# Eight experts in a written order, with whole-row gathers from a second copy of their input

## The chip, the core and the metric

The kernel runs on one NeuronCore of a Trainium2 chip. The metric is the device time of one execution in microseconds (us). The core has engines that each run their own queue of instructions: TensorE (PE in the profile; its weight loads are PEld), VectorE (DVE), ScalarE (ACT), GpSimd (POOL) and SyncE (SP), which here only issues DMAs. They wait for one another by semaphores. POOL issues the indirect DMAs, whose row numbers stand in SBUF.

## The reference

Block-causal attention over 4 x 8 heads of 576 x 64, a gated dense FFN on its 2304 rows of 512, and then eight experts. Everything is float32. The change touches the rows between the dense FFN and the output:

```python
def _moe2_ref(x, w_gate, w1, w2):          # x: 2304 x 512
    N, D = x.shape; E = w_gate.shape[1]    # E = 8
    cap = N // E                           # 288 tokens for an expert
    logits = x @ w_gate
    ...                                    # by falling logit: a token to the expert, while the expert has room
    out = np.zeros((N, D))
    for e in range(E):
        mask = assigned == e
        h = np.maximum(x[mask] @ w1[e], 0.0)   # 288 x 512 @ 512 x 1024
        out[mask] = h @ w2[e]                  # 288 x 1024 @ 1024 x 512
    return out
```

## The kernel before

Attention and the dense FFN's first half fill the span up to about 580 us, and the router, which decides the expert of every token, runs on DVE beside the FFN's second half. The FFN's second half (`A` of L683) leaves the experts' input, x2, as tiles `x2r`: ACT copies a group from PSUM with L690, and SP stores it by L692 to DRAM, in two arrays `x2_d[0]` and `x2_d[1]` of 2304 x 256, one for each half of a row. The last tiles hold one half row each, 128 x 256; so array 0 is complete one tile before array 1. When the router has written the table `idx`, the rows of an expert can be fetched.

**An expert** has 288 tokens, in pieces of 128, 128 and 32. `gather` (L997) fetches them with indirect DMAs on POOL, one per half row and piece: six for an expert. `xtrans` turns them on TensorE (L1009, three transposes for each of four slices `d` of the row) and splits each slice into a high part `exh{d}` (ACT, L1012) and a low part `exl{d}` (DVE); each product is made from three matmuls, high x high, low x high, high x low. The first layer has eight groups `f` (L1049), each of 12 matmuls with 288 columns, so 96 for an expert; ACT and DVE make `eh{f}` and `el{f}` of each. The second layer has four groups `d` of 24 (L1090), 96 too; ACT copies each to `yt{d}` (L1095). `ytrans` turns the four `yt` back on TensorE (L1023, 12 transposes), copies the three pieces to `yr` (ACT L1026, DVE L1028 twice), and sends them to their rows of the output with indirect DMAs on POOL (L1030).

The weights come in 64 loads through a ring (`eraw`, on SP's queue). `split` makes the high part `ewh` on ACT (L969) and the low part `ewl` in two halves, by turns on DVE (L974) and POOL (L976).

**Order.** `Experts.run` hands its instructions to a scheduler, which has its own estimates of costs and due times and may move an instruction ahead of others on its engine, within what the data allow. The first half of expert 0's slices (d = 0, 1) depends on `x2_d[0]` alone, and `early` starts five of its groups f with the six matmuls of these slices (30 in all, `EARLY`) ahead of the transposes for d = 2 and 3. The gathers of expert e+1 are written at the start of expert e. The transposes and scatters of expert e are the `tail` that is worked off beside the first layer of expert e+1.

Of the kernel before, what the change touches and what calls it, by code (L numbers as in the profile page):

```python
# [8 lines left out]
F32 = mybir.dt.float32  # L9
# [3 lines left out]
AF = mybir.ActivationFunctionType  # L13
OP = mybir.AluOpType
AX = mybir.AxisListType

P = 128
# [3 lines left out]
def f32(ap):  # L21
    return ap.bitcast(F32)
# [583 lines left out]
class Ffn2:  # L606
# [88 lines left out]
CAP = 288  # L695
# [228 lines left out]
        yield 0  # L924


EARLY = 5


class Experts:  # L930
# [27 lines left out]
    def split(self, eng):  # L958

        k, nc = self.k, self.k.nc  # L960
        if self.ns >= 64:
            return
        e, c = self.chunks[self.ns]
        self.ns += 1
        x = self.rawt.pop((e, c))
        h = self.ring.tile([P, 1024], F32R, name="ewh")
        l = self.ring.tile([P, 1024], F32R, name="ewl")
        self.w[e, c] = (h, l)
        nc.scalar.activation(h, x, AF.Copy)  # L969
        yield  # L970
        for a in range(2):
            s = slice(512 * a, 512 * a + 512)
            if eng == "v":
                nc.vector.tensor_tensor(l[:, s], x[:, s], f32(h[:, s]), op=OP.subtract)  # L974
            else:
                nc.gpsimd.tensor_tensor(l[:, s], x[:, s], f32(h[:, s]), op=OP.subtract)  # L976
            yield
        self.load()

# [4 lines left out]
    def open(self, st):  # L984
        tc = self.k.tc
        self.yg = st.enter_context(tc.tile_pool(name="yg", bufs=2))
        self.hb = st.enter_context(tc.tile_pool(name="ehb", bufs=1))

    def gather(self, e):
        k, nc = self.k, self.k.nc  # L990
        if e >= 8:
            return
        for c in range(2):
            for j, (a, b) in enumerate(self.TOK):
                if c == 0:
                    self.gx[e, j] = self.xg.tile([P, 512], F32, name=f"xg{j}")
                nc.gpsimd.indirect_dma_start(out=self.gx[e, j][0:b - a, 256 * c:256 * c + 256], out_offset=None, in_=k.x2_d[c][:, :],  # L997
                                             in_offset=bass.IndirectOffsetOnAxis(ap=k.idx[0:b - a, 3 * e + j:3 * e + j + 1], axis=0))

    def xtrans(self, e):  # L1000

        k, nc = self.k, self.k.nc
        if e >= 8:
            return
        parts = self.xt[e] = []
        for d in range(4):
            o = k.psA.tile([P, 512], F32, name="A")
            for j, (a, b) in enumerate(self.TOK):
                nc.tensor.transpose(o[:, a:b], self.gx[e, j][0:b - a, d * P:(d + 1) * P], k.ident[0:b - a, 0:b - a])  # L1009
            h = self.xg.tile([P, 288], F32R, name=f"exh{d}")  # L1010
            l = self.xg.tile([P, 288], F32R, name=f"exl{d}")
            nc.scalar.activation(h, o[:, 0:288], AF.Copy)  # L1012
            nc.vector.tensor_tensor(l, o[:, 0:288], f32(h), op=OP.subtract)
            parts.append((h, l))
            yield

    def ytrans(self, e, yt):
        k, nc = self.k, self.k.nc
        for j, (a, b) in enumerate(self.TOK):
            n = b - a  # L1020
            o = k.psA.tile([P, 512], F32, name="A")
            for d in range(4):
                nc.tensor.transpose(o[0:n, d * P:(d + 1) * P], yt[d][:, a:b], k.ident)  # L1023
            r = self.yg.tile([P, 512], F32, name=f"yr{j}")
            if j == 0:
                nc.scalar.activation(r[0:n], o[0:n], AF.Copy)  # L1026
            else:
                nc.vector.tensor_copy(r[0:n], o[0:n])  # L1028
            yield
            s = nc.gpsimd.indirect_dma_start(out=k.out[:, :], out_offset=bass.IndirectOffsetOnAxis(  # L1030
                ap=k.idx[0:n, 3 * e + j:3 * e + j + 1], axis=0), in_=r[0:n, :], in_offset=None)
            for x in self.sent:
                k.tc.declare_no_dep(s.ins, x.ins, reason="no token is in two slots")
            self.sent.append(s)
            yield

    def run(self):
        k, nc = self.k, self.k.nc
        nxt = self.xtrans(0)
        tail, bg = iter(()), iter(())  # L1040
        early = {}

        def first(o, e, f, ds):
# [8 lines left out]
        next(nxt)  # L1052
        for f in range(EARLY):
            early[f] = k.psF.tile([P, 512], F32, name="A")
            first(early[f], 0, f, (0, 1))
        drain(nxt)
        for e in range(8):
            self.gather(e + 1)
            hs = []
            for f in range(8):  # L1060
# [15 lines left out]
                next(bg, None)  # L1076
            yt = []
            nxt = self.xtrans(e + 1)
            for d in range(4):
                drain(bg)  # L1080
                bg = self.split("v" if d % 2 == 1 else "g")
                next(bg, None)
                wh, wl = self.w[e, 4 + d]
                o = k.psF.tile([P, 512], F32, name="A")
                n = 0
                for f in range(8):
                    s = slice(P * f, P * f + P)
                    h, l = hs[f]
                    for w, x in ((wh, h), (wh, l), (wl, h)):
                        nc.tensor.matmul(o[:, 0:288], w[:, s], x, start=(n == 0), stop=(n == 23))  # L1090
                        n += 1
                    if f in (3, 5):
# [4 lines left out]
                if d >= 1:  # L1097
                    next(nxt, None)
            drain(nxt)
            drain(tail)  # L1100
            tail = self.ytrans(e, yt)
            yield
        drain(tail)


# [4 lines left out]
def drain(g):  # L1110
    for _ in g:
        pass
# [54 lines left out]
def tile_fn(ctx, tc, q, kk, v, w_gate, w_val, w_out, m_gate, w1, w2, out, dbg=None):  # L1167
    nc = tc.nc
    nb = 4
    k = K()  # L1170
    k.nc, k.tc, k.ctx, k.q, k.kk, k.v, k.nb = nc, tc, ctx, q, kk, v, nb
    k.w_gate, k.w_val, k.w_out, k.m_gate, k.w1, k.w2, k.out = w_gate, w_val, w_out, m_gate, w1, w2, out
    dram = ctx.enter_context(tc.tile_pool(name="dram", bufs=1, space=bass.MemoryType.DRAM))
    k.h_d = [dram.tile([P, 12, 576], F32, name=f"h{b}") for b in range(nb)]
    k.wgv_d = dram.tile([12, 2, P, 512], F32, name="wgv")
    k.wo_d = dram.tile([12, P, 512], F32, name="wo32")
    k.x2_d = [dram.tile([2304, 256], F32, name=f"x2d{c}") for c in range(2)]
# [28 lines left out]
    ex = Experts()  # L1206
# [10 lines left out]
    with tc.manual_schedule():  # L1217
        n = 0
# [46 lines left out]
```

## Time and profile before

| | us |
|---|---|
| three runs | 1047.32, 1046.84, 1045.98 (median 1046.84) |
| profiled execution | 1045.71 |
| its span, first to last instruction | 1044.0 |
| PE busy | 993.2 (95%) |
| DVE, ACT, POOL busy | 587.7, 449.7, 507.4 |
| mean granted clock of TensorE, as a share of full | 0.985 |

How to read it: the span and what lies around it (1.7 us) make the profiled execution's time. TensorE is busy nearly throughout, so the places that matter are those where it isn't, or where it is busy at a lower granted clock. Nearly the whole stretch from 785 us to the end belongs to the experts. In a row of the timeline, the bracket at the end holds the time that the engine was idle just before, and what ended it: an engine, tile and line, a DMA, "remote" (something that the profile couldn't place) or "issue" (nothing that the profile shows).

### The profile page before, as it was taken

What the parts mean: (1) busy time and instruction counts of PE and PEld (TensorE: products, weight loads), DVE (VectorE), ACT (ScalarE), POOL (GpSimd) and SP (SyncE); (2) the same over time, 40 slices, a digit from 0 to 9 for tenths busy, and PEclk for the clock granted to TensorE, in tenths of its full rate; (3) what the DMA queues carried; (4) which work ended last, traced back from release to release, by engine and by line L of the source; (5) the groups of instructions that cost most, each with busy time, mean ns of one, the idle gap of its engine ahead of it and who ended that gap; (6) DMA issues with size and microseconds to landing.
All of it is one profiled execution on the core that took longest, in us unless ns stands there. A gap on an engine that the chain in (4) does not pass through costs nothing.

```text
span 1044.0 us, 19724 instructions
## 1 busy us (share of the span) xinstructions
PE 993.2 (95%) x7387; PEld 858.1 (82%) x7387; DVE 587.7 (56%) x1385; ACT 449.7 (43%) x1069; POOL 507.4 (49%) x519
## 2 busy tenths in 40 slices
PE   7979999999999999999999999999997999999995
PEld 4658888788888888899999766666687999999995
DVE  5887889477666455435685566655631434434441
ACT  5765565355554455434554222111121444444541
POOL 3663444433333334532324677765645666666441
PEclk9989999999999999998999999999998999999998
DMA  6556666556454322236665543433312665555540
GB/s 170 141 130 176 203 199 178 181 165 185 142 184 119 96 68 79 75 98 226 207 210 157 148 126 102 119 84 96 98 47 63 205 186 174 177 169 183 185 127 23
DMA packets 188527, 148.89 MB, mean 143 GB/s; under 512 B 70800, under 2 KB 161424, under 8 KB 188432
## 3 DMA queue, kind: packets, MB, share of 16 engines
q1 hardware_dynamic: 184848, 138.20, 44.5%
q0 software_dynamic: 3584, 9.44, 2.8%
q8 instruction: 58, 0.95, 0.4%
q14 instruction: 37, 0.30, 0.1%
HBM read 114.57 MB, written 33.03 MB: 141 GB/s over the span
## 4 chain that ended last, share of the span: by engine, by line
PE 84%; DVE 8%; issue 4%; POOL 1%; ACT 1%; SPq 1%; DMA 0%; POOLq 0%; another core or an unknown queue 0%; ACTq 0%; DVEq 0%
PE A L457 29%; PE A L683 12%; PE A L1049 10%; PE A L1090 9%; PE A L211 5%; PE A L116 4%; PE A L163 4%; PE A L824 2%; PE A L410 2%; DVE sub L811 2%; PE A L122 2%; PE A L1009 1%; PE A L85 1%; DVE cmp L840 1%; DVE hl L512 1%
## 5 line engine op out<-in xcount | busy, mean ns | idle before, releaser
L151 POOL TENSOR_SCALAR p<-p,stat 128x128 f32<-128x128 f32 (+2 forms) x144 | 81.2, 576 | 191.1 <-DVE stat L149 135.8
L359 POOL TENSOR_TENSOR w0l<-wf,w0h 128x512 fp32r<-128x512 f32 x48 | 67.0, 1395 | 136.9 <-ACT w0h L357 103.4
L457 PE MATMUL A<-xh,w0h 128*128 128x288 f32 x384 | 121.6, 317 | 2.6 <-ACT w0h L357 2.6
L457 PE MATMUL A<-xh,w1h 128*128 128x288 f32 x384 | 122.1, 318 | 1.9 <-ACT ptb L168 1.9
L976 POOL TENSOR_TENSOR ewl<-eraw,ewh 128x512 fp32r<-128x512 f32 x68 | 90.2, 1345 | 63.1 <-ACT ewh L969 55.6
L457 PE MATMUL A<-xh,w0l 128*128 128x288 f32 x384 | 114.5, 298 | 3.7 <-POOL w0l L359 3.7
L457 PE MATMUL A<-xh,w1l 128*128 128x288 f32 x384 | 114.3, 298 | 0.0
L457 PE MATMUL A<-xl,w1h 128*128 128x288 f32 x384 | 114.3, 298 | 0.0
L457 PE MATMUL A<-xl,w0h 128*128 128x288 f32 x384 | 114.1, 297 | 0.0
L969 ACT ACTIVATE ewh<-eraw 128x1024 fp32r<-128x1024 f32 x64 | 67.8, 1060 | 67.2 <-PE A L1090 42.0
L124 DVE TENSOR_REDUCE stat<-A 128x1 f32<-128x128 f32 (+4 forms) x160 | 70.4, 477 | 44.2 <-PE A L122 20.5
L683 PE MATMUL A<-wo_h,hl 128*128 128x512 f32 (+1 forms) x240 | 95.0, 396 | 0.0
L683 PE MATMUL A<-wo_l,hh 128*128 128x512 f32 (+1 forms) x240 | 92.1, 384 | 0.0
L660 POOL TENSOR_TENSOR hl<-hraw,hh 128x512 fp32r<-128x512 f32 x54 | 75.8, 1426 | 28.7 <-ACT hh L656 28.7
L683 PE MATMUL A<-wo_h,hh 128*128 128x512 f32 (+1 forms) x240 | 89.7, 374 | 0.0
L974 DVE TENSOR_TENSOR ewl<-eraw,ewh 128x512 fp32r<-128x512 f32 x60 | 48.6, 851 | 70.8 <-ACT ewh L969 64.9
L138 ACT ACTIVATE p<-A,stat 128x128 f32<-128x128 f32 (+4 forms) x160 | 81.8, 520 | 11.7 <-DVE stat L124 7.5
L690 ACT ACTIVATE x2r<-A 128x512 f32<-128x512 f32 (+1 forms) x20 | 11.1, 555 | 168.2 <-PE A L683 162.6
L1049 PE MATMUL A<-exh,ewh 128*128 128x288 f32 x256 | 75.9, 314 | 6.0 <-issue 3.3
L457 PEld LDWEIGHTS A<-xh,w1h 128*128 128x128 f32 x384 | 73.5, 191 | 9.0 <-issue 5.1
L457 PEld LDWEIGHTS A<-xh,w0h 128*128 128x128 f32 x384 | 73.1, 190 | 8.7 <-issue 4.4
L1049 PE MATMUL A<-exl,ewh 128*128 128x288 f32 x256 | 75.8, 299 | 2.3 <-issue 2.3
(219 smaller groups left out, 2717.1 us busy)
## 6 DMA issues: line engine op xcount, KB each, us to landing
eraw<-in_moe_w_dram SPq DMA_DIRECT2D x64, 512.0 KB, 3.9
wf<-wgv SPq DMA_DIRECT2D x72, 256.0 KB, 3.0
h<-h SPq DMA_DIRECT2D x48, 288.0 KB, 2.7
hraw<-h SPq DMA_DIRECT2D x16, 768.0 KB, 5.2
hraw<-h SPq DMA_DIRECT2D x12, 576.0 KB, 4.0
w<-in_moe_w_gate_dram SPq DMA_DIRECT2D x12, 512.0 KB, 4.3
w<-in_moe_w_val_dram SPq DMA_DIRECT2D x12, 512.0 KB, 4.1
wgv<-wf SPq DMA_DIRECT2D x24, 256.0 KB, 4.3
```

Of the source, the lines that this page charges most:

```text
L124: nc.vector.tensor_reduce(st[:, x:x + 1], s[:, 0:w], axis=AX.X, op=OP.max, negate=True)
L138: nc.scalar.activation(o, s[:, 0:w], AF.Exp, bias=m, scale=1.0, accum_out=st[:, 2 + x:3 + x])
L151: self.k.mark = nc.gpsimd.tensor_scalar(t, t, r[:, x:x + 1], 1.0, op0=OP.mult, op1=OP.mult)
L211: nc.tensor.matmul(o[64 * a:64 * a + 64, b0:w], vs[0:kk, c, a, :], th[0:kk, a, c, b0:w], start=(n == 0), stop=(n == len(mm) - 1))
L359: nc.gpsimd.tensor_tensor(l, x, f32(h), op=OP.subtract)
L457: nc.tensor.matmul(o[:, 0:288], w[:, ks], x[:, ts], start=(kk == 0 and n == 0), stop=(kk == 3 and n == 2))
L660: nc.gpsimd.tensor_tensor(l[:, s], x[:, s], f32(h[:, s]), op=OP.subtract)
L683: nc.tensor.matmul(o[:, 0:b - a], x[:, f], w[:, f, a:b], start=(f == 0 and n == 0), stop=(f == 11 and n == 2))
L969: nc.scalar.activation(h, x, AF.Copy)
L976: nc.gpsimd.tensor_tensor(l[:, s], x[:, s], f32(h[:, s]), op=OP.subtract)
L1049: nc.tensor.matmul(o[:, 0:288], w[:, s], x, start=(d == 0 and n == 0), stop=(d == 3 and n == 2))
L1090: nc.tensor.matmul(o[:, 0:288], w[:, s], x, start=(n == 0), stop=(n == 23))
```

## The change

- Each tile `x2r` is stored twice: by halves to `x2_h[0]`, `x2_h[1]` (the former `x2_d`), and whole to the new `x2_d` of 2304 x 512.
- Only expert 0 is gathered by halves, six DMAs. Experts 1 to 7 are gathered by whole rows, three DMAs each.
- `EARLY` is 6: 36 matmuls of expert 0 go ahead of the transposes of its slices 2 and 3.
- The experts run under `manual_schedule`: every engine gets its instructions as they are written. So the groups f are no longer interleaved, the four transposes of a piece stand together behind the groups f = 0, 1, 2, and the three transposes of a slice for the next expert stand behind the 12th matmul of a group d.
- The weight splits have new places: five of eight on DVE and three on POOL, before four and four.
- `rows` takes the place of `ytrans`. A memset of one element on POOL stands between the scatters of a piece. For the last expert, the transposes of yt0 to yt2 with their copies (384 columns) go into the middle of the last group d; behind the last matmul come three transposes, copies of 128 columns and the scatters.

```diff
-                nc.sync.dma_start(k.x2_d[c // 256][t * P:(t + 1) * P, :], y[:, c - a:c - a + 256])
+                nc.sync.dma_start(k.x2_h[c // 256][t * P:(t + 1) * P, :], y[:, c - a:c - a + 256])
+            nc.sync.dma_start(k.x2_d[t * P:(t + 1) * P, a:b], y[:, 0:b - a])
...
-EARLY = 5
+EARLY = 6
...
-        for c in range(2):
+        self.gx[e] = [self.xg.tile([P, 512], F32, name=f"xg{j}") for j in range(3)]
+        for src in k.x2_h if e == 0 else (k.x2_d,):
             for j, (a, b) in enumerate(self.TOK):
...
+                g = self.gx[e][j][0:b - a]
+                if e == 0:
+                    c = k.x2_h.index(src)
+                    g = g[:, 256 * c:256 * c + 256]
+                nc.gpsimd.indirect_dma_start(out=g, out_offset=None, in_=src[:, :],
...
-    def ytrans(self, e, yt):
+    def rows(self, e, yt, ds, copies):
...
+        lo, hi = ds[0] * P, ds[-1] * P + P
         for j, (a, b) in enumerate(self.TOK):
+            o = self.yo[j]
+            for d in ds:
+                nc.tensor.transpose(o[0:b - a, d * P:(d + 1) * P], yt[d][:, a:b], k.ident)
+            r = self.yr[j][0:b - a]
             if j == 0:
+                nc.scalar.activation(r[:, lo:hi], o[0:b - a, lo:hi], AF.Copy)
             else:
+                nc.vector.tensor_copy(r[:, lo:hi], o[0:b - a, lo:hi])
+            if copies:
+                if j:
+                    nc.gpsimd.memset(self.one, 0.0)
+                s = nc.gpsimd.indirect_dma_start(out=k.out[:, :], ...
...
             for f in range(8):
+                if f % 2 == 0:
+                    drain(bg)
+                    if e or f:
+                        bg = self.split("vg"[f // 2 % 2])
+                    next(bg, None)
...
-                if f % 2 == 1:
-                    drain(bg)
-                    bg = self.split("v" if f % 4 == 1 else "g")
...
-                bg = self.split("v" if d % 2 == 1 else "g")
+                bg = self.split("gv"[d % 2] if d else "v")
...
+                    if f == 3:
+                        next(nxt, None)
+                        if e == 7 and d == 3:
+                            drain(self.rows(e, yt, (0, 1, 2), False))
...
-            tail = self.ytrans(e, yt)
-            yield
+            tail = self.rows(e, yt, range(4) if e < 7 else (3,), True)
...
-    ex.gather(0)
-    drain(ex.run())
+    with tc.manual_schedule():
+        ex.gather(0)
+        ex.run()
```

What follows are pieces of the engines' orders; a name with its number is one tile. First POOL before, from the start of the gathers: x2d_63 and x2d_64 are the arrays of the first and of the second half row; xg_9782, 9784 and 9786 are the pieces of expert 0, xg_9858, 9860 and 9862 those of expert 1.

```order
L997 DMA xg_9782<-x2d_63,idx 128x256
L997 DMA xg_9784<-x2d_63,idx 128x256
L997 DMA xg_9786<-x2d_63,idx 32x256
L997 DMA xg_9858<-x2d_63,idx 128x256
L997 DMA xg_9860<-x2d_63,idx 128x256
L997 DMA xg_9862<-x2d_63,idx 32x256
L997 DMA xg_9782<-x2d_64,idx 128x256
L997 DMA xg_9784<-x2d_64,idx 128x256
L997 DMA xg_9786<-x2d_64,idx 32x256
L997 DMA xg_9858<-x2d_64,idx 128x256
```

And the same place now, with x2h_64 and x2h_65 for the halves and x2d for the whole rows; xg_9806 to 9808 are expert 0's, xg_9889 to 9891 expert 1's:

```order
L1000 DMA xg_9806<-x2h_64,idx 128x256
L1000 DMA xg_9807<-x2h_64,idx 128x256
L1000 DMA xg_9808<-x2h_64,idx 32x256
L1000 DMA xg_9806<-x2h_65,idx 128x256
L1000 DMA xg_9807<-x2h_65,idx 128x256
L1000 DMA xg_9808<-x2h_65,idx 32x256
L1000 DMA xg_9889<-x2d,idx 128x512
L1000 DMA xg_9890<-x2d,idx 128x512
L1000 DMA xg_9891<-x2d,idx 32x512
L974 TENSOR_TENSOR ewl<-eraw,ewh 128x512 x6
```

Expert 0's second halves have moved ahead of all of expert 1's; and the 18 gathers that stood in a row (six more for expert 2 behind those shown) have become nine, with expert 0's six weight halves between them and expert 2's.

POOL before at the start of an expert (expert 1; gathers for the expert after the next one's start, then the scatters of the expert that has ended):

```order
L997 DMA xg_10527<-x2d_63,idx 128x256
L997 DMA xg_10527<-x2d_64,idx 128x256
L997 DMA xg_10529<-x2d_63,idx 128x256
L997 DMA xg_10531<-x2d_63,idx 32x256
L997 DMA xg_10529<-x2d_64,idx 128x256
L997 DMA xg_10531<-x2d_64,idx 32x256
L1030 DMA out_dram<-yr_10193,idx 2304x512
L1030 DMA out_dram<-yr_10240,idx 2304x512
L976 TENSOR_TENSOR ewl<-eraw,ewh 128x512 x2
L1030 DMA out_dram<-yr_10289,idx 2304x512
L976 TENSOR_TENSOR ewl<-eraw,ewh 128x512 x6
```

And now:

```order
L1000 DMA xg_10542<-x2d,idx 128x512
L1000 DMA xg_10543<-x2d,idx 128x512
L1000 DMA xg_10544<-x2d,idx 32x512
L1040 DMA out_dram<-yr_10571,idx 2304x512
L1039 MEMSET one 1x1
L1040 DMA out_dram<-yr_10572,idx 2304x512
L1039 MEMSET one 1x1
L1040 DMA out_dram<-yr_10573,idx 2304x512
L974 TENSOR_TENSOR ewl<-eraw,ewh 128x512 x6
```

Eight indirect DMAs in a row have become four, then one and one with a memset ahead of each, and the weight halves all stand behind the third scatter.

TensorE at the end of the program before, from the last matmuls of expert 7 on:

```order
L1090 MATMUL A_12610<-el7_12525,ewh_12490 128x288
L1090 MATMUL A_12610<-eh7_12524,ewl_12491 128x288
L1023 MATMUL A_12637<-ident_71,yt0_12554 128x128
L1023 MATMUL A_12637<-ident_71,yt1_12581 128x128
L1023 MATMUL A_12637<-ident_71,yt2_12608 128x128
...
L1023 MATMUL A_12637<-ident_71,yt3_12635 128x128
L1023 MATMUL A_12645<-ident_71,yt3_12635 128x128
L1023 MATMUL A_12653<-ident_71,yt3_12635 32x128
```

And now:

```order
L1031 MATMUL A_12642<-ident_72,yt0_12571 32x128
L1031 MATMUL A_12642<-ident_72,yt1_12598 32x128
L1031 MATMUL A_12642<-ident_72,yt2_12625 32x128
L1107 MATMUL A_12627<-eh4_12484,ewh_12507 128x288
...
L1107 MATMUL A_12627<-eh7_12541,ewl_12508 128x288
L1031 MATMUL A_12640<-ident_72,yt3_12670 128x128
L1031 MATMUL A_12641<-ident_72,yt3_12670 128x128
L1031 MATMUL A_12642<-ident_72,yt3_12670 32x128
```

Nine of the twelve transposes have moved from behind the last matmul to 12 matmuls ahead of it.

## Rows read from the trace of the kernel before

**Rows 1.** Two stretches: busy PE, PEld, DVE, ACT, POOL; granted clock; DMA share; GB/s.
```profile
780.00:800.00 20.00, 15.09 (x99) 14.17 (x98) 1.74 (x4) 2.31 (x6) 13.43 (x16) 0.88 0.28 85
1004.00:1031.00 27.00, 27.00 (x204) 26.68 (x205) 9.00 (x18) 9.39 (x19) 5.36 (x5) 1.00 0.20 62
```

**Rows 2.** Timeline of TensorE around the start.
```profile
784.33 0.28 PE L683 MATMUL A<-wo_h,hl 128*128 128x256 f32 x1
784.46 1.10 PE L1009 MATMUL A<-ident,xg 128*128 128x128 f32 x6
...
794.86 0.62 PE L1009 MATMUL A<-ident,xg 128*128 128x128 f32 x4
```

**Rows 3.** Timeline of ACT around the start: start, us, instruction, idle before.
```profile
780.38 0.39 ACT L690 ACTIVATE x2r<-A 128x256 f32<-128x256 f32 x1 [3.93 <-PE A L683]
786.34 0.38 ACT L690 ACTIVATE x2r<-A 128x256 f32<-128x256 f32 x1 [5.57 <-PE A L1009]
787.78 0.71 ACT L1012 ACTIVATE exh<-A 128x288 fp32r<-128x288 f32 x2 [1.06 <-remote]
797.23 0.41 ACT L1012 ACTIVATE exh<-A 128x288 fp32r<-128x288 f32 x1 [8.74 <-remote]
```

**Rows 4.** The chain that ended last, first layer of expert 0: start, us, what.
```profile
788.25 5.76 PE A L1049 x30
...
795.48 2.22 issue
797.70 6.80 PE A L1049 x37
804.50 0.52 issue
...
805.31 0.40 issue
...
808.87 4.28 PE A L1090 x32
```

**Rows 5.** Timeline of POOL: gathers at the start, and expert 1's run of eight.
```profile
779.07 1.20 POOL L997 DMA_INDIRECT xg<-x2d,idx  x1 [8.08 <-DMA x2d<-x2r]
...
785.53 0.87 POOL L997 DMA_INDIRECT xg<-x2d,idx  x1 [0.30 <-issue]
788.71 0.97 POOL L997 DMA_INDIRECT xg<-x2d,idx  x1 [2.31 <-DMA x2d<-x2r]
...
853.82 0.99 POOL L997 DMA_INDIRECT xg<-x2d,idx  x1 [1.00 <-PE A L1009]
```

**Rows 6.** Timeline of ACT during that run of eight.
```profile
857.20 0.60 ACT L1026 ACTIVATE yr<-A 128x512 f32<-128x512 f32 x1 [2.40 <-issue]
...
861.02 0.41 ACT L1069 ACTIVATE eh<-A 128x288 fp32r<-128x288 f32 x1 [3.22 <-PE A L1049]
```

**Rows 7.** The same chain, experts 1, 6 and 7.
```profile
823.80 0.99 PE A L1049 x6
...
975.60 0.99 PE A L1049 x6
...
985.02 4.74 PE A L1049 x36
...
1004.68 0.99 PE A L1049 x6
```

**Rows 8.** All x2 stores of L692, from issue to landing.
```profile
DMA to landing us min/median/max: 1.7/1.8/2.7
```

**Rows 9.** All gathers of L997, in ns (min/median/max).
```profile
L997 POOL DMA_INDIRECT xg<-x2d,idx x48: 864/954/1314, 779.1 to 951.6; - x48
```

**Rows 10.** Timeline of all engines behind the last matmul.
```profile
1031.63 1.47 PE L1023 MATMUL A<-ident,yt 128*128 128x128 f32 x12
1032.92 0.60 ACT L1026 ACTIVATE yr<-A 128x512 f32<-128x512 f32 x1 [0.62 <-PE A L1023]
...
1033.79 0.99 POOL L1030 DMA_INDIRECT out_dram<-yr,idx  x1 [16.68 <-ACT yr L1026]
```

More of the change, by code (lines that the diff above doesn't have):

```diff
@@ L972, in split @@
             s = slice(512 * a, 512 * a + 512)
[L973 to L976, printed above, removed]
+            (nc.vector if eng == "v" else nc.gpsimd).tensor_tensor(l[:, s], x[:, s], f32(h[:, s]), op=OP.subtract)
             yield
@@ L987, in open @@
         self.hb = st.enter_context(tc.tile_pool(name="ehb", bufs=1))
+        self.one = self.hb.tile([1, 1], F32, name="one")
     def gather(self, e):
@@ L992, in gather @@
             return
-        for c in range(2):
+        self.gx[e] = [self.xg.tile([P, 512], F32, name=f"xg{j}") for j in range(3)]
+        for src in k.x2_h if e == 0 else (k.x2_d,):
             for j, (a, b) in enumerate(self.TOK):
-                if c == 0:
-                    self.gx[e, j] = self.xg.tile([P, 512], F32, name=f"xg{j}")
-                nc.gpsimd.indirect_dma_start(out=self.gx[e, j][0:b - a, 256 * c:256 * c + 256], out_offset=None, in_=k.x2_d[c][:, :],
+                g = self.gx[e][j][0:b - a]
[3 more added lines that the diff above has]
+                nc.gpsimd.indirect_dma_start(out=g, out_offset=None, in_=src[:, :],
                                              in_offset=bass.IndirectOffsetOnAxis(ap=k.idx[0:b - a, 3 * e + j:3 * e + j + 1], axis=0))
@@ L1008, in xtrans @@
             for j, (a, b) in enumerate(self.TOK):
-                nc.tensor.transpose(o[:, a:b], self.gx[e, j][0:b - a, d * P:(d + 1) * P], k.ident[0:b - a, 0:b - a])
+                nc.tensor.transpose(o[:, a:b], self.gx[e][j][0:b - a, d * P:(d + 1) * P], k.ident[0:b - a, 0:b - a])
             h = self.xg.tile([P, 288], F32R, name=f"exh{d}")
@@ L1015, in xtrans @@
             yield
-    def ytrans(self, e, yt):
+    def rows(self, e, yt, ds, copies):
         k, nc = self.k, self.k.nc
+        if not self.yo:
+            self.yo = [k.psA.tile([P, 512], F32, name="A") for _ in self.TOK]
+            self.yr = [self.yg.tile([P, 512], F32, name=f"yr{j}") for j in range(3)]
+        lo, hi = ds[0] * P, ds[-1] * P + P
         for j, (a, b) in enumerate(self.TOK):
[L1020 to L1024, printed above, removed]
+            o = self.yo[j]
+            for d in ds:
+                nc.tensor.transpose(o[0:b - a, d * P:(d + 1) * P], yt[d][:, a:b], k.ident)
+            r = self.yr[j][0:b - a]
             if j == 0:
-                nc.scalar.activation(r[0:n], o[0:n], AF.Copy)
+                nc.scalar.activation(r[:, lo:hi], o[0:b - a, lo:hi], AF.Copy)
             else:
-                nc.vector.tensor_copy(r[0:n], o[0:n])
-            yield
[L1030 to L1034, printed above, removed]
-            yield
+                nc.vector.tensor_copy(r[:, lo:hi], o[0:b - a, lo:hi])
+            if copies:
+                if j:
+                    nc.gpsimd.memset(self.one, 0.0)
+                s = nc.gpsimd.indirect_dma_start(out=k.out[:, :], out_offset=bass.IndirectOffsetOnAxis(
+                    ap=k.idx[0:b - a, 3 * e + j:3 * e + j + 1], axis=0), in_=r, in_offset=None)
+                for x in self.sent:
+                    k.tc.declare_no_dep(s.ins, x.ins, reason="no token is in two slots")
+                self.sent.append(s)
+            yield
+        if copies:
+            self.yo = []
     def run(self):
         k, nc = self.k, self.k.nc
+        self.yo = []
         nxt = self.xtrans(0)
-        tail, bg = iter(()), iter(())
+        tail = iter(())
         early = {}
@@ L1059, in run @@
             hs = []
+            bg = iter(())
             for f in range(8):
+                if f % 2 == 0:
[3 more added lines that the diff above has]
+                    next(bg, None)
                 if f in early:
@@ L1072, in run @@
                 next(tail, None)
-                if f % 2 == 1:
-                    drain(bg)
-                    bg = self.split("v" if f % 4 == 1 else "g")
                 next(bg, None)
+            drain(tail)
             yt = []
@@ L1091, in run @@
                         n += 1
-                    if f in (3, 5):
+                    if f in (1, 5):
                         next(bg, None)
+                    if f == 3:
+                        next(nxt, None)
+                        if e == 7 and d == 3:
+                            drain(self.rows(e, yt, (0, 1, 2), False))
                 y = self.hb.tile([P, 288], F32, name=f"yt{d}")
@@ L1096, in run @@
                 yt.append(y)
-                if d >= 1:
-                    next(nxt, None)
+            drain(bg)
             drain(nxt)
-            drain(tail)
-            tail = self.ytrans(e, yt)
-            yield
+            tail = self.rows(e, yt, range(4) if e < 7 else (3,), True)
         drain(tail)
@@ L1176, in tile_fn @@
     k.wo_d = dram.tile([12, P, 512], F32, name="wo32")
-    k.x2_d = [dram.tile([2304, 256], F32, name=f"x2d{c}") for c in range(2)]
+    k.x2_d = dram.tile([2304, 512], F32, name="x2d")
+    k.x2_h = [dram.tile([2304, 256], F32, name=f"x2h{c}") for c in range(2)]
     const = k.const = ctx.enter_context(tc.tile_pool(name="const", bufs=1))
```

## The prediction

> **What bounds the kernel now.** I read three views: busy time by stretches, the chain of waits from the experts' start to the end, and the timelines of ACT and POOL where that chain leaves TensorE. From 1004 to 1031, the last expert, TensorE is busy 27.00 of 27.00 us at granted clock 1.00; between 780 and 800 it is busy 15.09 of 20 at 0.88 [rows 1]. So an expert in full swing is bound by TensorE itself, and time can be had at the start, in what makes experts 1 to 5 slower than expert 6, and behind the last matmul.
>
> The start: the last matmul of the dense FFN ends at 784.6 [rows 2]. ACT's x2r before it came at 780.38; the last one should follow at 784.7 and comes at 786.34, with ACT idle for 5.57 [rows 3]. TensorE gets to the experts at 788.25, waits 2.22 at 795.48, and has two gaps later (0.52, 0.40); the first layer ends at 808.87 [rows 4]. Both waits are odd. Transposes end at 795.48, but ACT's exh follows at 797.23, and the profile names no releaser ("remote") [rows 2, 3]. Each time POOL is deep in a run of indirect DMAs with 0.30 between two: the first six run from 779.07 to 786.40, the moment at which x2r moves; twelve more begin at 788.71 [rows 5]. I read from it that **after some five indirect DMAs in an unbroken run, TensorE's signals reach the other engines 1 to 2.7 us late**, and TensorE is held up too.
>
> The same in the middle: expert 1's run of eight begins at 853.82 [rows 5]. ACT's yr at 857.20, 3.4 into it, has 2.40 of idle; eh at 861.02, 7.2 into it, has 3.22 [rows 6]. Experts 1 to 5 take (975.60 - 823.80) / 5 = 30.36 each; expert 6, which gathers nothing (there is no expert 8), takes 29.08 [rows 7].
>
> **The change, part by part.** The sum is made against the profiled execution, 1045.71.
>
> *T1, the start to the end of expert 0's first layer.* POOL now issues three gathers and waits for the second half's last store. They end at 779.07 + 3 x 1.25 = 782.8, so POOL rests when the FFN ends: x2r at 784.7, stored from 785.1 instead of 786.72. The transposes' signal is prompt too: exh0 at 785.1 to 785.5, then exl0, which the written order now asks for with the second matmul (before, exh alone was used first): stream from 786.0. 36 early matmuls at full clock take 4.74, 0.132 each [rows 7]: 790.7. [...] The second half: its store goes 1.62 earlier, so its gathers too, from 788.71 [rows 5] to 787.1; the third is issued by 790.5 and lands about 1.1 later (an estimate, from 1.8 between issue and landing of a store [rows 8] less its own 0.9 in a gather's issue), 791.6. Six transposes (0.6) and the split of a slice (0.4 + 0.4): second layer-halves from 792.6. That leaves a wait of about 1.3 apart from the transposes. Then 96 - 36 = 60 matmuls x 0.132 = 7.9, 800.5; I keep the two later gaps (0.92), since six gathers still stand in a run there: about 801.5, so **T1 = 801.5 - 808.87 = -7.4**. Bounds: if nothing becomes prompt, only the sixth group is gained (six matmuls, 0.8, that fill part of the 2.22): -0.8; without the gaps kept, -8.3.
>
> *T2, expert 0's second layer* (808.87 to 823.80 [rows 4, 7]): the same matmuls and transposes, 0 (0 to -0.3).
>
> *T3, experts 1 to 5.* POOL's run at an expert's start falls from eight to four (three whole-row gathers, one scatter), some 5 us, then single scatters with a memset ahead of each. A whole-row gather fetches as many rows as a half-row one, each twice as long; I price it as before, 954 ns in the middle [rows 9]; the trace has no gather of 2 KB rows but scatters of such rows, 0.99 each [rows 10]. If all the excess over expert 6 goes: 5 x 29.08 - 151.80 = -6.4. I take -5.5, since a run of four still reaches five us. Below: nothing, 0, if the run isn't the cause. Matmuls and transposes are equal in number. Strict order is covered: ahead of the first group's use of exh3 stand 12 matmuls of d = 3 and nine of the group, 21 x 0.132 = 2.8, against 0.8 for ACT and DVE. POOL's split written at f = 2 stands behind the third scatter, which waits for the copy of the third piece behind f = 2 (36 matmuls and 12 transposes, 4.7 + 1.5 [rows 7, 10]); with copy, scatter and 2.6 for two halves it is done some 11 us into the expert, and its weights are used in d = 1, 96 x 0.132 + 1.5 + 3.5 = 17.7 into it. The memsets ride in that slack.
>
> [...]
>
> *T4, the tail.* Nine of the last 12 transposes move ahead of 12 matmuls. All 12 took 1.47 [rows 10], so nine put 1.0 into the stream before its end: +1.0. Behind the last matmul yt3's copy is as before; the first scatter came 1033.79 - 1032.92 = 0.87 after the copy of 512 columns (0.60) began [rows 10]. 128 columns should take 0.3: -0.3. yt3's copy starts when the last matmul ends whatever stood behind it, and nine transposes lay beside that copy before; so they were hidden: -0.2 for the shorter way to yt3. **T4 = +0.5** (from -0.3 to +1.0).
>
> *The second copy of x2* adds 20 DMAs on SP's queue in the FFN's second half, each behind the half stores of its tile, beside a TensorE that bounds that stretch: 0, and the first whole-row gather asks for it only after six others. Upward bound +0.3 for the last tile's extra issue.
>
> **Sum:** -7.4 + 0 - 5.5 + 0.5 = -12.4, so 1033.3 for an execution like the profiled one. That one is 1.13 under the median of the runs; predicted: **1034.4**.
>
> **Rivals.** *R1: the lateness comes with the gathers' bytes or with any indirect DMA, not with an unbroken run.* For it: the same bytes move at the same places. Against: expert 6, whose POOL has scatters only, has no excess, and expert 1's ACT is prompt 3.4 into the run. Then -0.8 + 0 + 0.5: 1046.5, no change.
>
> *R2: half the gain.* In the new start POOL still runs six gathers in a row (three second halves, three of expert 1) from 787.1 to 794.5, and the split of slice 2 falls at 792.6, 5.5 into it; x2r was late 5.6 into its run. So exh comes 2 late, the wait of 1.3 becomes 3.3 and the clock falls again: 37 matmuls took 6.80 after the wait of 2.22 [rows 4], 1.9 over 37 x 0.132. T1 is then -7.4 + 2 + 1.9 = -3.5; with T3 at -3 (a run of four still disturbs), 1045.71 - 6.0 + 1.13 = 1040.8. [...]
>
> *R3: slower, by the written order.* The scheduler could fill a hole with another group's matmuls; the written order can't. The place is the first product with the low part of the last slice, or the weights of d = 1 behind the third scatter: it decides if the former is over 2.0 late (2.8 - 0.8) or POOL over 6 late. Price: a stall of 2 us as at 795.48, once in each of seven experts, +14: 1048.4. For it: ACT and DVE were put in order by that same scheduler. Against: the last expert needed no such help at 27.00 of 27.00.
>
> **How the numbers follow.** Forecast 0.62, R2 0.22, R1 0.09, R3 0.07. The forecast's own range is 1031.4 (all lower bounds, -15.3) to 1038. R2 reaches to 1042; beyond lie R1 and R3. Range 1031 to 1042. A measurement of this kernel can't tell less than 0.2% (2.1 us) from no change. Faster: forecast and R2, 0.84; same: R1 and a little, 0.09; slower 0.07.
>
> **What would show it.** Of the changed kernel: x2r's last copy within 0.2 of the last FFN matmul; the experts' first matmul some 1.4 behind it, at clock 1.00; a wait of one to two at the second transposes (over 3: R2); expert 0's first layer ending 16 to 17 behind the FFN; experts 1 to 5 at 29.1 to 29.4, like expert 6; ACT's idle at eh under 2.5 us. Periods of 30 would show R1, stalls at a first-layer group's ninth matmul or at d = 1 R3. The last scatter should begin as long after the last matmul as before less half a microsecond.

## The result, and the profile after

The changed kernel took 1035.24 us (median of 1036.99, 1034.03, 1035.24), the ratio to the kernel before is 0.9895, interval 0.9874 to 0.9917. The forecast was 1034.4. The profiled execution is the 1036.99 one, its span 1034.8. Its dense FFN ends at 787.46, 2.85 later than before [rows 2]. Up to there the change only adds the second stores of x2, and two other executions of the same kernel, in the experiments, end it at 785.03 and 784.95. So I count from the end of the last FFN matmul: 259.35 us to the end of the span before, 247.31 now, 12.0 less.

The chain of waits of the changed kernel (start, us, what); L1062 is the first layer, L1107 the second, L1012 the transposes of x2:

```profile
787.55 0.39 ACT x2r L690
...
788.32 2.53 DMA x2d<-x2r
...
793.77 2.13 DMA xg<-x2h,idx
...
796.81 9.84 PE A L1062 x60
806.65 1.58 PE A L1107 x12
...
821.81 1.60 PE A L1062 x12
...
967.82 1.58 PE A L1062 x12
...
996.95 1.60 PE A L1062 x12
```

The chain names the whole-row store (`x2d<-x2r`) ahead of the second half's gathers because it lands last, at 790.85; POOL's last wait there was for the half store, which landed at 790.41.

The first layer of expert 0 ends 806.65 - 787.46 = 19.19 behind the FFN; it was 24.26 [rows 2, 4]. Experts 1 to 5 take 967.82 - 821.81 = 146.01, 29.20 each, as expert 6 does (29.13); they took 151.80 [rows 7]. The "issue" gaps of the first layer are gone. ACT is prompt at the start, its idle at x2r is 3.93 instead of 5.57 [rows 3] (timeline of ACT):

```profile
787.55 0.38 ACT L690 ACTIVATE x2r<-A 128x256 f32<-128x256 f32 x1 [3.93 <-PE A L683]
787.89 0.95 ACT L1015 ACTIVATE exh<-A 128x288 fp32r<-128x288 f32 x2
```

What is left of the start is a wait for the gathers of the second half, and the clock behind it (busy time by stretches: PE, PEld, DVE, ACT, POOL, granted clock, DMA share, GB/s; by stretches of 2 us the granted clock is 1.00 up to 796, then 0.72, 0.50 and 0.93, and 1.00 again from 802):

```profile
794.00:798.00 4.00, 2.60 (x10) 1.70 (x11) 0.92 (x2) 0.82 (x2) 3.09 (x4) 0.86 0.40 114
798.00:802.00 4.00, 4.00 (x24) 4.00 (x24) 0.92 (x2) 2.10 (x5) 0.58 (x2) 0.71 0.22 75
```

The end (timeline; L1116 is yt's copy, L1031 the last three transposes, L1034 yr's copy, L1040 the scatters):

```profile
1024.53 0.30 PE L1107 MATMUL A<-eh,ewl 128*128 128x288 f32 x1
1024.92 0.41 ACT L1116 ACTIVATE yt<-A 128x288 f32<-128x288 f32 x1 [1.81 <-PE A L1107]
1025.38 0.55 PE L1031 MATMUL A<-ident,yt 128*128 128x128 f32 x3 [0.56 <-ACT yt L1116]
1025.75 0.28 ACT L1034 ACTIVATE yr<-A 128x128 f32<-128x128 f32 x1 [0.42 <-PE A L1031]
1026.30 1.00 POOL L1040 DMA_INDIRECT out_dram<-yr,idx  x1 [14.44 <-ACT yr L1034]
```

The copy of 128 columns takes 0.28 where 512 took 0.60 [rows 10]. POOL's queue closes with a DRAIN, which is 2.5 us shorter now (8.54 before, 6.00). Its end lies 4.24 behind the end of the last scatter; it was 5.95. The closing instructions of POOL's queue (duration in ns min/median/max), first of the kernel before, then of the changed one:

```profile
L1261 POOLq DRAIN x3: 46/102/8542, 1034.6 to 1043.7; - x3
```

```profile
L1281 POOLq DRAIN x3: 46/102/6002, 1028.0 to 1034.5; - x3
```

The following table is worked out from the starts and ends of the matmuls in each trace. The columns: from the end of the last FFN matmul to the first matmul of expert 0's second layer (the chain above counts some 0.16 more); the rest of expert 0 (its second layer); experts 1 to 5; 6; 7; from the last matmul to the end of the span; their sum. The last five rows belong to the experiments.

| kernel, chip | first layer | second | 1 to 5 | 6 | 7 | end | sum |
|---|---|---|---|---|---|---|---|
| before | 24.09 | 15.03 | 151.80 | 29.07 | 27.18 | 12.17 | 259.35 |
| changed | 19.03 | 15.15 | 146.01 | 29.13 | 28.04 | 9.95 | 247.31 |
| before, chip B | 23.36 | 15.61 | 151.16 | 29.07 | 27.19 | 12.17 | 258.56 |
| changed, chip B | 18.94 | 15.17 | 146.01 | 29.13 | 28.04 | 9.95 | 247.25 |
| before, chip C | 16.76 | 15.02 | 145.79 | 29.07 | 27.19 | 12.18 | 246.01 |
| changed, chip C | 18.72 | 15.16 | 146.01 | 29.13 | 28.04 | 9.95 | 247.00 |
| best (last run), chip C | 16.44 | 15.18 | 146.01 | 29.13 | 27.07 | 10.27 | 244.09 |

### The profile page after: what moved, and what is told of

Same layout as the page of the kernel before. It is cut to its first block, busy times and chain, and to the rows that moved or that the text cites. A ratio compares the mean times of both kernels' runs of the same rounds, so it can differ in the third digit from the quotient of the medians.

```text
span 1034.8 us, 19695 instructions
## 1 busy us (share of the span) xinstructions
PE 990.2 (96%) x7387; PEld 854.5 (83%) x7387; DVE 594.6 (57%) x1399; ACT 456.1 (44%) x1070; POOL 477.1 (46%) x502
## 4 chain that ended last, share of the span: by engine, by line
PE 82%; DVE 8%; DMA 3%; issue 3%; POOL 2%; ACT 1%; SPq 1%; POOLq 0%; ACTq 0%; DVEq 0%
PE A L457 27%; PE A L683 12%; PE A L1062 9%; PE A L1107 9%; PE A L211 5%; PE A L116 4%; PE A L163 4%; PE A L825 2%; PE A L410 2%; DVE sub L812 2%; PE A L122 2%; PE A L85 1%; DVE cmp L841 1%; PE A L1012 1%; DMA hraw<-h 1%
## 5 line engine op out<-in xcount | busy, mean ns | idle before, releaser
L974 POOL TENSOR_TENSOR ewl<-eraw,ewh 128x512 fp32r<-128x512 f32 x56 | 75.3, 1363 | 71.5 <-ACT ewh L970 71.3
L1107 PE MATMUL A<-eh,ewh 128*128 128x288 f32 x256 | 78.5, 307 | 0.0
L1062 PE MATMUL A<-exh,ewh 128*128 128x288 f32 x256 | 78.1, 305 | 0.0
L470 DVE SCALAR_TENSOR_TENSOR h<-sg,A 128x288 f32<-128x288 f32 x96 | 43.0, 448 | 58.3 <-PE A L457 41.3
L1062 PE MATMUL A<-exl,ewh 128*128 128x288 f32 x256 | 76.3, 298 | 0.1
```

The source lines that it names most:

```text
L470: nc.vector.scalar_tensor_tensor(h[:, ts], sg, 1.0, ps[1][:, 0:288], op0=OP.add, op1=OP.mult)
L974: (nc.vector if eng == "v" else nc.gpsimd).tensor_tensor(l[:, s], x[:, s], f32(h[:, s]), op=OP.subtract)
L1062: nc.tensor.matmul(o[:, 0:288], w[:, s], x, start=(d == 0 and n == 0), stop=(d == 3 and n == 2))
```

## The experiments

They were run in three sets of four, each on another chip; I call the chips A, B and C. Beside each set the kernel before ran as its reference: 1033.34 us on A (21 runs, 1031.48 to 1035.13), 1047.47 on B (13 runs, 1045.82 to 1049.90), 1033.60 on C (31 runs, 1031.44 to 1036.64). That is the largest finding of the study, and it came from the references: **the kernel before is 14 us faster on A and C than on B, without any edit.**

### Chip A: runs of gathers, and the order

First: six half-row gathers for every expert, all else as changed.

```diff
-        for src in k.x2_h if e == 0 else (k.x2_d,):
+        for src in k.x2_h:
```

> The changed kernel, but with six half-row gathers for every expert (the second copy is still stored). If an unbroken run of indirect DMAs makes TensorE's signals late, the run of six gathers (some 7.3 us) and the scatter behind it bring the lateness back: ACT's or DVE's idle at eh and el of the second or third group 1 us longer, gaps of TensorE near 0.5 to 1.2 in each of experts 1 to 5, periods of 29.7 to 30.4 instead of 29.2, and 1038 to 1042 us in all. If the written order was what helped, periods stay at 29.2 and the time within 1.5 of 1035.2.

It took 1037.02, 1.0036 (1.0023 to 1.0048) of the kernel before. The periods are 29.24, 29.13, 29.25, 29.13, 29.25: no late signals at all, though nine gathers stand in a row at the start. It tells nothing of the theory, since on this chip the kernel before takes 1033.34 and has nothing to lose to late signals. But it shows what the gathers' number costs: with the changed kernel's own tail, its end is 11.66 against 9.95, and POOL's closing DRAIN is

```profile
L1281 POOLq DRAIN x3: 46/102/7717, 1026.3 to 1034.6; - x3
```

7.72 with 72 indirect DMAs in the program against 6.00 with 51: 1.71 for 21 of them.

Second: the same with a memset ahead of each gather.

```diff
+                nc.gpsimd.memset(self.one, 0.0)
                 nc.gpsimd.indirect_dma_start(out=g, ...
```

> As the run before, with a memset of one element on POOL ahead of every gather; bytes and number of indirect DMAs as there. If only an unbroken run makes signals late, the periods go back to 29.2 and the time to 1034.5 to 1037 (the memsets cost POOL 0.1 to 0.3 each, hidden but at the start). If lateness belongs to the number of indirect DMAs, it is as slow as the run before, 1038 to 1042.

1041.01, 1.0075 (1.0059 to 1.0092): slower, and for a reason outside both theories. The first memset waits for the FFN's last matmul, since its one element lies in a pool that takes over the FFN's memory; the first gathers wait behind it, and TensorE gets to the experts 7.17 behind the FFN instead of 0.90 (timeline of POOL):

```profile
786.65 0.09 POOL L1000 MEMSET one<- 1x1 f32 x1 [13.68 <-PE A L683]
787.61 1.20 POOL L1001 DMA_INDIRECT xg<-x2h,idx  x1 [0.87 <-issue]
```

Periods 29.25 and 29.13 as in the first run. Whether a memset breaks a run where signals do come late is open.

Third: the kernel before with only the second copy and whole-row gathers for experts 1 to 7.

```diff
+            nc.sync.dma_start(k.x2_w[t * P:(t + 1) * P, a:b], y[:, 0:b - a])
...
-        for c in range(2):
+        for c in range(2 if e == 0 else 1):
```

> The kernel before with the second copy of x2 and whole-row gathers for experts 1 to 7; the scheduler's order, five early groups and the tail as before. POOL's run at an expert's start falls from eight to five (6.2 us). By the theory of unbroken runs it has most of the gain: periods of 29.3 to 29.8, the start 4 to 6 shorter, 1036 to 1040 in all. By the rival, that the written order makes the gain, it stays at 1043 to 1047.

1032.53, 0.9994 (0.9982 to 1.0006). Fourth: the changed kernel without its written order.

```diff
-    with tc.manual_schedule():
-        ex.gather(0)
-        ex.run()
+    ex.gather(0)
+    ex.run()
```

> The changed kernel, ordered by the scheduler instead of as written (the memsets move away from the scatters, which stand three in a row; gathers three in a row). By the theory of unbroken runs periods of 29.1 to 29.4 and 1034 to 1037.5. By the rival, that the written order makes the gain, periods of 29.8 or more and over 1039.

1034.51, 1.0007 (0.9997 to 1.0016), periods 29.29 and 29.14, beside 29.25 and 29.13 for the written order. I had read the reference's 1033.34 as a puzzle until the next set: both kernels equal the kernel before because here it has nothing to lose. The changed kernel itself was not run on A.

### Chip B: where signals come late

The two kernels again, unchanged:

> The kernel before, unchanged, on the chip on which the variants are timed. If the late signals belong to the order of its indirect DMAs, they stand here as in its first trace: experts 1 to 5 at 30 to 30.8 us, first layer of expert 0 ending 24 behind the FFN, some 1.1% slower than the changed kernel. If they belong to the chip or to one execution, the periods are 29.2 here.

> The changed kernel, unchanged, as a control beside the others: periods of 29.2, first layer of expert 0 ending 19.0 behind the FFN, last matmul to the end 10.0.

Before took 1048.24 (1.0003, 0.9992 to 1.0015), changed 1033.88: 0.9878 (0.9862 to 0.9894). Of these 14.4 us the places of the table hold 11.3; in the two traces the FFN ends at 788.88 and 785.03, and why it ends later in the kernel before isn't known. The old pattern stands in the trace of before, ACT at the start and in expert 1's run of eight:

```profile
790.59 0.38 ACT L690 ACTIVATE x2r<-A 128x256 f32<-128x256 f32 x1 [5.56 <-PE A L1009]
...
864.49 0.41 ACT L1069 ACTIVATE eh<-A 128x288 fp32r<-128x288 f32 x1 [3.24 <-PE A L1049]
```

Then the changed kernel with half-row gathers, no memsets, and the scheduler's order, which puts 18 gathers in a row at the start (six, a wait, twelve) and runs of six in the middle:

```diff
-        for src in k.x2_h if e == 0 else (k.x2_d,):
+        for src in k.x2_h:
...
-                if j:
-                    nc.gpsimd.memset(self.one, 0.0)
...
-    with tc.manual_schedule():
```

> The changed kernel with half-row gathers for every expert, no memsets, and the scheduler's order. POOL's start is again 18 gathers in a row with the halves of experts 0 and 1 interleaved; in the middle the run is six gathers, weight halves, three scatters. Theory of the long run at the start: first layer ends 22 to 25 behind the FFN with exh 1.5 to 2.7 late, as before; middle at 29.2 to 29.6, since six were harmless in written order. Rival, that eight DMAs in a row with scatters among them make signals late, whatever the gathers: start as in the changed kernel (19 to 21) and middle 29.2.

1042.76, 0.9958 (0.9941 to 0.9975). The start is late as before: TensorE reaches the experts 3.65 behind the FFN, the first layer ends at 25.72. ACT's timeline there:

```profile
787.20 0.38 ACT L690 ACTIVATE x2r<-A 128x256 f32<-128x256 f32 x1 [5.61 <-PE A L1012]
...
807.99 0.41 ACT L1086 ACTIVATE eh<-A 128x288 fp32r<-128x288 f32 x1 [9.23 <-remote]
```

In the middle the periods are 29.27, 29.14, 29.29, 29.14, 29.29: runs of six cost no time there. Signals are late in them all the same. The `eh` of each expert's third group begins 1.31 to 1.39 behind the group's last matmul in all five experts, some 7.5 us into the run; in the fourth run, with the same scheduler and gathers in threes (on chip A), it begins 0.04 behind it in all five. ACT's rows of expert 2, first of this run, then of the fourth:

```profile
863.07 0.41 ACT L1086 ACTIVATE eh<-A 128x288 fp32r<-128x288 f32 x1 [1.61 <-PE A L1031]
```

```profile
854.82 0.41 ACT L1088 ACTIVATE eh<-A 128x288 fp32r<-128x288 f32 x1 [0.36 <-PE A L1062]
```

So on this chip, in one trace, signals are late in the long run and in the runs of six, and only the first costs time. The run makes three edits at once: what the half rows alone bring back on B, without the scheduler's order and with the memsets, isn't shown.

The eighth run tried to keep the clock up in the second wait (behind it the changed kernel on this chip has 0.57 from 794 to 798), with 16 matmuls of no use:

```diff
+        junk = k.psA.tile([P, 512], F32, name="A")
+        for n in range(16):
+            nc.tensor.matmul(junk[:, 0:288], self.w[0, 0][0][:, 0:P], self.xt[0][0][0], start=True, stop=True)
         drain(nxt)
```

> The changed kernel with 16 matmuls of no use, into a PSUM bank that nothing reads, between the early groups and the second transposes of expert 0, where TensorE waited about 2.9 us in pieces. If the 1.9 us that the 60 matmuls behind the wait lost are the clock's fall after idleness, the first layer ends 1.5 to 2 earlier (17.1 to 17.6 behind the FFN) and the clock stays at 1.00. If the fall has another cause, or the 16 matmuls hold up the transposes, it ends at 19.0 to 19.8.

1035.01, 0.9883 (0.9866 to 0.9899); the first layer ends at 21.59, 2.7 later than in the changed kernel, at a clock of 0.97 from 794 to 798 and 0.60 from 798 to 802: the opposite of what was hoped, and of use for that. Of this kernel, POOL's run of six, TensorE's transposes and ACT's answer, from the timelines of the three engines:

```profile
788.27 0.96 POOL L1000 DMA_INDIRECT xg<-x2h,idx  x1 [5.58 <-DMA x2d<-x2r]
...
792.91 0.55 PE L1012 MATMUL A<-ident,xg 128*128 128x128 f32 x3
794.00 0.61 PE L1012 MATMUL A<-ident,xg 128*128 128x128 f32 x3 [0.54 <-PE A L1012]
...
794.72 0.41 ACT L1015 ACTIVATE exh<-A 128x288 fp32r<-128x288 f32 x1 [8.79 <-PE A L1012]
796.17 0.41 ACT L1015 ACTIVATE exh<-A 128x288 fp32r<-128x288 f32 x1 [1.03 <-remote]
```

And the changed kernel on the same chip, its transposes and ACT's answer, in a run of six from 788.61:

```profile
792.67 0.33 PE L1012 MATMUL A<-ident,xg 128*128 128x128 f32 x1 [0.92 <-DMA xg<-x2h,idx]
793.39 0.79 PE L1012 MATMUL A<-ident,xg 32*128 32x32 f32 x4 [0.40 <-DMA xg<-x2h,idx]
...
793.67 0.95 ACT L1015 ACTIVATE exh<-A 128x288 fp32r<-128x288 f32 x2 [7.24 <-PE A L1012]
```

In the eighth run the first three transposes end at 793.46, 5.2 into the run, and ACT follows 1.26 later; the second three end at 794.61 and ACT follows at 796.17, "remote". In the changed kernel the last transpose ends at 794.18, 5.6 into its run, and ACT, which does both slices in one stretch from 793.67 to 794.62, waits for nothing. So in this run of six signals came late, as rival R2 said; but the time into the run doesn't decide alone, as I had it. What differs is TensorE: in the eighth run it streamed without a pause from the early groups through the 16 matmuls to the transposes, in the changed kernel it had rested 0.92 and 0.40 for the gathers within the run. In the long run of the kernel before (788.25 to 795.48 in the first trace), and in the middle of the seventh run (825.02 to 845.12 around expert 1's six gathers), it streams too. Whether the rest is what keeps the signals prompt wasn't tried.

### Chip C: both kernels where nothing is late, and a better one

> The kernel before, unchanged. The reference beside the first four variants took 1033 on one chip, beside the next four 1047 on another. If late signals belong to some chips, this trace shows either the old pattern (1046 to 1049, x2r 1.7 late, experts 1 to 5 at 30 to 30.8) or none of it (1031 to 1035, stream 1.0 behind the FFN, periods 29.1 to 29.2), nothing between. If it varied from execution to execution, the rounds would hold both.

1032.92, 0.9995 (0.9985 to 1.0006). The same program as in the fifth run, and none of the pattern. Its POOL in the run of eight, and its ACT:

```profile
847.08 0.99 POOL L997 DMA_INDIRECT xg<-x2d,idx  x1 [1.00 <-PE A L1009]
...
856.20 0.99 POOL L1030 DMA_INDIRECT out_dram<-yr,idx  x1 [0.30 <-DVE el L1070]
```

```profile
786.12 0.38 ACT L690 ACTIVATE x2r<-A 128x256 f32<-128x256 f32 x1 [3.94 <-PE A L683]
...
852.82 0.41 ACT L1069 ACTIVATE eh<-A 128x288 fp32r<-128x288 f32 x1 [1.75 <-PE A L1049]
```

The run is as long as before, eh comes 5.74 into it, at 1.75 of idle; in [rows 6] it came 7.2 in with 3.22. x2r follows the FFN in 0.09.

The traces also hold the times of the semaphore updates themselves. TensorE's update that lets the last x2r begin stands at 786.27 in the first trace of the kernel before, where the last FFN matmul ends at 784.62; here it stands at 786.05, and the matmul ends at 786.04. So what is late is TensorE's signal and not ACT. (The profile models the ends of matmuls, so a matmul that was itself held up would look the same.)

> The changed kernel, unchanged, beside it: 1033 to 1036 on either chip; so 1.2% faster than before where signals come late, and within 0.3% of it where they don't.

1034.08, 1.0009 (0.9996 to 1.0022): no gain. In the table's rows for chip C the changed kernel is 1.0 behind: first layer +1.96, expert 0's second layer and experts 1 to 6 together +0.42, the last expert +0.85, the end -2.23.

> The kernel before with the second copy and whole-row gathers only (as in the third run). Where signals come late from 5.2 us into a run: the start has nine gathers in a row, so exh of slice 2, asked for 5.1 into it, may be just prompt and eh of the first groups late by 1 to 2; runs of five in the middle (6.2 us) touch little, periods of 29.2 to 29.6; 1032 to 1037 in all, most of the change's gain. Where no signal comes late: 1032.5.

1032.82, 0.9990 (0.9978 to 1.0002); it landed on a chip where it can't answer its question, what whole rows alone give where signals come late, and that stays open. It answers another one. It is the third run's kernel, whose first layer ended at 17.10, and here at 18.79. Busy time and clock in the 4 us behind the wait, first of the third run, then of this one:

```profile
794.00:798.00 4.00, 3.56 (x26) 3.45 (x27) 0.82 (x2) 0.71 (x2) 2.95 (x4) 1.00 0.49 148
```

```profile
794.00:798.00 4.00, 3.59 (x15) 3.59 (x16) 0.82 (x2) 0.66 (x2) 3.09 (x4) 0.57 0.54 153
```

The same instructions in the same order: 26 matmuls at clock 1.00 or 15 at 0.57. The two executions were on different chips, and the second's gather starts 3.70 behind the FFN instead of 3.53, so the 1.7 us between them are the clock's fall and 0.17 of a longer wait. How long TensorE idles doesn't decide alone: between 790 and 798 it idles 1.91 in the third run and 2.13 here, but on C also 1.56 in the kernel before, at clock 1.00, and 1.38 in the changed one, whose clock falls to 0.59.

The last run makes three edits to the changed kernel: the sixth early group stands between the pieces of the second transposes; the whole-row stores of the last two tiles go behind both half stores, so that the wait which the gather's own instruction carries is that for the last half store; and the tail is in one part.

```diff
-        for f in range(EARLY):
+        for f in range(EARLY - 1):
...
+        for j, (a, b) in enumerate(self.TOK):
+            for d in (2, 3):
+                nc.tensor.transpose(os[d - 2][:, a:b], ...
+            if j == 0:
+                ...
+                first(early[f], 0, f, (0, 1))
...
+            elif (t, a) == (17, 256):
+                for u in (16, 17):
+                    nc.sync.dma_start(k.x2_d[u * P:(u + 1) * P, :], last[u])
...
-                        if e == 7 and d == 3:
-                            drain(self.rows(e, yt, (0, 1, 2), False))
```

> The changed kernel with three edits: the sixth early group stands between the pieces of the second transposes (it breaks the wait, so the clock should stay at 1.00, 1.9 us); the last stores of the whole rows go behind both last half stores, so the last half store is the one that the gather itself waits for (the gather 0.7 to 1.1 earlier); one-part tail (0.35). In all 2 to 4 us faster than the changed kernel, 1030 to 1033. If the wait's length or the clock is set elsewhere, 0.3 faster at most.

1031.59, 0.9974 (0.9963 to 0.9986) of the kernel before, where the changed one beside it has 1.0009: it beats both on this chip, by 1.3 us (2.0 against the reference's 1033.60) and 2.5 us. Its first second-half gather and the matmuls behind the wait, POOL's timeline and busy time:

```profile
788.79 0.96 POOL L1011 DMA_INDIRECT xg<-x2h,idx  x1 [4.38 <-DMA x2h<-x2r]
```

```profile
794.00:798.00 4.00, 3.59 (x25) 3.38 (x26) 1.74 (x4) 2.42 (x6) 1.57 (x3) 1.00 0.47 148
```

FFN's end to this gather is 2.56 (786.23 to 788.79), in the changed kernel on this chip 3.58; that is 1.0. With it and the clock at 1.00 the first layer ends at 16.44 instead of 18.72; whether the clock holds in every execution, and whether the moved group holds it, one trace can't say. The one-part tail gives 27.07 + 10.27 = 37.34 against 28.04 + 9.95 = 37.99. On a chip with late signals it wasn't tried.

## Why the prediction was right, and where it wasn't

The sum, -12.4 against -12.0 measured by places, is right for the chip of the first pair, which the record doesn't name, and nearly for B (-11.3). That it is so close is in part luck: T1 missed by 2.3 one way, T4 by 1.9 the other. The sizes of three terms were off, and one assumption under all of them didn't hold everywhere. (The lowest bounds, -15.3, give 1031.5 and not 1031.4.)

*T3, experts 1 to 5*: -5.5 forecast, -5.79 measured. The reading that the excess over expert 6 (30.36 against 29.08) is lost in the run of eight fits: without that run it is gone. A run of four was not tried, since in the trace three gathers stand together and the scatter comes some 2.5 us later. Chip C shows the other side: there the old run of eight loses none either, and the two kernels' periods differ by 0.04 to 0.06, in favour of the old one.

*T1, the start*: -7.4 forecast, -5.1 measured. x2r and exh are prompt as forecast, the stream starts 0.9 behind the FFN (forecast 1.4). The step that was mis-sized is the second half: I put its gathers 2.5 behind the FFN's end, from the distance of store and gather in the trace before; they start 3.8 behind it (787.46 to 791.25). The semaphore records split these 1.3: the last half store lands 2.46 after its issue instead of 1.70 (on C, in the kernel before, 2.49), and the gather starts 0.84 after the landing instead of 0.26. The third, fourth, tenth and eleventh runs, in which POOL waits for that store in an instruction of its own too, have 0.83 to 0.84; where the gather carries the wait itself, in the kernel before and in the last run, it is 0.26. So the second halves start at 9.3 instead of 8.0, and then 60 matmuls take 9.84 instead of 7.9 and two gaps: the clock fell behind the wait (0.50 from 798 to 800), which I had priced only in R2. The gaps that I kept didn't come. That the 36 early matmuls run at full clock from the start, 4.74, was my estimate from expert 6 [rows 7], and nothing in the trace before shows it for this place; in the changed kernel the clock is 1.00 from 788 to 794 and they take 5.51 (788.36 to 793.87), the first six 1.40 and the other 30 at 0.132 each. The 1.1 that I put from a gather's issue to its landing is more than the 1.8 less 0.9 it was made from; the third gather of the second halves landed 2.13 after its start, 1.26 after its end.

*T4, the end*: +0.5 forecast, -1.4 measured. The nine transposes cost 0.86 in the stream (1.0 forecast), and the last scatter starts 4.05 behind the last matmul instead of 4.57 (forecast half a microsecond less). What I left out is POOL's closing DRAIN: 21 fewer gathers shorten it, and with it the end, by 1.71.

*T2*: 0 forecast, +0.1 measured. The second copy was put at 0, at most +0.3, and costs about 0.6 at the start, the 0.84 in place of 0.26 above.

*The rivals.* R1, no gain, came true on C (1.0009), and on A the changed kernel under the scheduler gained nothing either (1.0007), though not by R1's mechanism: bytes and indirect DMAs are the same on all, and late signals are on some. R2 came true in the eighth run alone: its place (the split of slice 2, 5.2 into a run of six), a lateness of 1.3 to 1.6 and the clock's fall behind it (0.60); the changed kernel was spared the lateness, but not the clock's fall (0.57 in the sixth run, on the same chip). R3 didn't happen: the written order is no slower than the scheduler's in the fourth run (29.25 and 29.13 against 29.29 and 29.14), so the 0.04 to 0.06 an expert must lie elsewhere in the change.

The assumption that failed is that a wait seen in one trace of a program belongs to the program. The long run explains most of what B shows: signals late in runs of twelve, eight and six, with those of six in the middle costing no time. But in a run of six at the start they were late in the eighth run and prompt in the changed kernel, at nearly the same time into it, so TensorE's own stream may have a part in it. And it is no more than a condition: on A and C runs of nine, twelve and eight bring no lateness. What distinguishes the chips stays open; it may be the chip or what it was doing at the time. Each held its time through all its runs. One more difference is on record. The trace of the changed kernel on C holds 8832 semaphore updates by landings for its 552 DMAs, 16 each. Of the 8848 that this makes for the 553 of the kernel before, the trace on C holds 8838, the one on B 7984 and the first 7965; of the changed kernel's 8832, B's trace holds 8577 and the first 8605. So records are missing on the chips where signals come late, of the changed kernel too, and most of the slower one. All times here come with a recorded span and clock; whether the recording itself has a part in the lateness wasn't tried.

## What to carry to other kernels

The waits whose releaser had long been done, marked "remote" or "issue" while POOL issued DMAs 0.30 apart, stood in the kernel before on B and not on C, at 1047.47 and 1033.60 us: run the unchanged kernel on a second chip before a change is built against it, and compare variants only with a reference of the same chip. The change that removes them was worth 1.2% on B (0.9878) and nothing on C (1.0009), where its side costs (a wait with a clock of 0.59 behind it, 0.85 more in the last expert) are all that is left. Where TensorE must wait, it is worth trying a small group of ready matmuls in the middle of the wait instead of ahead of it: the last run, which does so, kept its clock at 1.00, though the third run on A and the kernel before on C kept 1.00 without.

## What was not expected of the hardware

- The end of POOL's queue was longer with more indirect DMAs in the whole program: the closing DRAIN ended 5.95 us behind the last scatter's end with 72 and 4.24 with 51, whether the tail was the old one or the new one.
- The same kernel, same order, kept clock 1.00 behind a wait in which TensorE idled 1.91 in one trace and had 0.57 behind 2.13 in another, the first layer 1.7 us apart.
- From a store's issue to the gather that waits for it took 1.96 in the kernel before and 3.3 in the changed one: 0.76 more to the landing, 0.58 more from the landing to the gather, whose wait stood in a separate instruction.
